# A gate column loaded as rows and turned by TensorE, and a re-searched order of operations, in a fused two-branch attention kernel

## The chip, the cores and the metric

One core of a Trainium2 chip. The metric is the device time of one execution in microseconds (us); the profile's span is about 1.7 us shorter than the time of the same execution. The profile shows five engines, and the program gives each its own fixed list of instructions: TensorE (PE, with its weight loads PEld), VectorE (DVE), ScalarE (ACT), GpSimd (POOL) and SyncE (SP), which issues most of this program's DMA. The lists are tied together by semaphores, and from these the profile infers what an engine waited for. A run counts as slow when it is over 1.5% above the fastest of its kernel in the same set; all others are called fast.

## The reference, cut to what matters

```
x = A_x                                            # 1 x 2048 x 640, bf16
g = sigmoid((x * gate_w).sum(-1, keepdims=True))   # one gate per token
a = A(x)   # linear attention, feature map softmax(+-x w), 32 heads of 20
b = B(x)   # 4 segments of 512 tokens: causal softmax attention + memory
return g * a + (1 - g) * b
```

The sum over `x * gate_w` is one more output column of a matrix product with x. The kernel therefore keeps `gate_w` as column 641 behind the 640 columns of the B branch's value weights.

## The kernel before

The program doesn't list its instructions in order. It builds a graph of some 1460 operations, each with its engine, an assumed duration and a priority, and a list scheduler in the same file turns the graph into one fixed order per engine and hands out PSUM banks. A table of offsets, found by a search, shifts the priorities:

```
NUDGE = {6: 1.6, 7: 1.65, 8: -2.2, ... 1450: -5.4}          # 417 entries (cut)
...
o.pr = pr + NUDGE.get(len(self.ops), 0.0)
...
# schedule(): per engine, among what is ready, the lowest priority number
# of those that could start within DELTA of the earliest
ch = min(((o.pr, o.idx, s, o) for s, o in cands if s <= lim))
```

The gate column was loaded by GpSimd, element by element, after the weight loads of B (`after=[last]`) and, in GpSimd's order, behind the building of masks:

```
self.WvB = fx("WvB", [128, NCH, D + 1], BF16)
...
self.dma("sp", self.WvB[:, :, 0:D], wsrc(ins["B_wv"]), W=[(self.WvB, "w")], pr=-760, dur=0.6, lat=5.6, name="WvB")
...
self.dma("pool", self.WvB[:, :, D:D + 1], ins["gate_w"].rearrange("(c p o) -> p c o", p=128, o=1),
         W=[(self.WvB, "g")], pr=-40, lat=6.0, noncontig=True, name="gw", after=[last])
```

and it is used by the value projection of each 128 tokens, whose operation reads both parts of the tile:

```
for kc in range(NCH):
    l = xT[:, kc, 128 * t:128 * (t + 1)]
    e.matmul(self.pf(pt, 0, 0, 512), lhsT=l, rhs=self.WvB[:, kc, 0:512], ...)
    r = e.matmul(self.pf(pt, 1, 0, 129), lhsT=l, rhs=self.WvB[:, kc, 512:641], ...)
```

The softmax here doesn't subtract the row's maximum and nothing guards it: scores larger than these inputs give would overflow.

## Time and profile before

| | before |
|---|---|
| time, median of the first 3 runs (range) | 337.8 us (336.91 to 338.0) |
| span of the profiled run | 334.1 us |
| TensorE busy / without a matmul | 303.6 / 30.5 us |
| VectorE, ScalarE busy | 244.5, 258.2 us |

"Without a matmul" is the span less TensorE's busy time. It is the quantity to watch, because both kernels do the same matmuls but one. The lines of the profile are shown in the prediction.

### The profile page before, as it was taken

The numbers are of one execution on the slowest core, as the hardware profiler recorded it, in microseconds if no ns is written. First come the engines' busy times: TensorE is split into PE (matmuls) and PEld (weight loads), VectorE is DVE, ScalarE is ACT, GpSimd is POOL, SyncE is SP. The second block draws the span as 40 slices with busy tenths as digits, with TensorE's granted clock in tenths as the row PEclk, the third lists the DMA queues.
The fourth block names the chain that finished last, engine by engine and source line by source line (L and its number), as shares of the span: only waits on it lengthen the run. The fifth ranks groups of instructions, "written<-read, shape, count | busy, mean of one in ns | idle before, by whom it ended". The sixth has DMA issues, their size and how long they took to land.

```text
span 334.1 us, 8947 instructions
## 1 busy us (share of the span) xinstructions
PE 303.6 (91%) x3836; PEld 176.2 (53%) x3836; DVE 244.5 (73%) x485; ACT 258.2 (77%) x325; POOL 114.8 (34%) x170
## 2 busy tenths in 40 slices
PE   7978999999987998899889999999999998889996
PEld 3434555476554545565454554664654655465763
DVE  4425898999999979899969798463792728667640
ACT  3448988978897898998977999768979776965522
POOL 6528323321434325642532114143221433322300
PEclk9999999999999999999999999999999999999999
DMA  7999992753722739650584104732014331210011
GB/s 248 302 142 222 81 146 56 79 119 57 104 39 45 117 54 88 122 97 2 121 157 41 22 1 62 129 70 61 22 22 57 84 59 33 50 42 22 22 41 59
DMA packets 68823, 27.52 MB, mean 82 GB/s; under 512 B 60400, under 2 KB 66864, under 8 KB 68784
## 3 DMA queue, kind: packets, MB, share of 16 engines
q1 hardware_dynamic: 68688, 26.92, 45.9%
q8 instruction: 30, 0.49, 0.6%
q0 software_dynamic: 96, 0.04, 0.3%
q14 instruction: 9, 0.07, 0.1%
HBM read 7.57 MB, written 4.59 MB: 36 GB/s over the span
## 4 chain that ended last, share of the span: by engine, by line
PE 45%; ACT 25%; DVE 15%; POOL 6%; DMA 6%; issue 2%; POOLq 0%; DVEq 0%
PE ps L1339 10%; ACT expT L999 6%; PE ps L1049 6%; ACT expT L1010 5%; PE ps L848 5%; ACT ET L1243 4%; POOL expT L1004 4%; PE ps L1136 4%; PE ps L989 3%; ACT expT L1022 3%; DMA WvB<-in_gate_w_dram 3%; PE ps L1238 3%; PE ps L1340 3%; PE ps L869 2%; DMA TT<-E 2%; ACT E L1143 2%
## 5 line engine op out<-in xcount | busy, mean ns | idle before, releaser
L1004 POOL TENSOR_SCALAR_AFFINE_SELECT expT<-expT 128x512 bf16<-128x512 bf16 x128 | 96.2, 754 | 187.4 <-ACT expT L999 80.8
L999 ACT ACTIVATE expT<-ps 128x1024 bf16<-128x1024 f32 x64 | 61.7, 1024 | 12.1 <-PE ps L989 11.7
L1010 ACT ACTIVATE expT<-ps 128x2048 bf16<-128x2048 f32 x32 | 60.0, 1875 | 4.9 <-PE ps L989 4.7
L1049 PE MATMUL ps<-v1B,expT 128*128 128x42 bf16 (+1 forms) x1280 | 42.3, 181 | 4.5 <-POOL expT L1004 2.7
L1049 PEld LDWEIGHTS ps<-v1B,expT 128*128 128x128 bf16 x1280 | 38.5, 96 | 12.5 <-POOL expT L1004 4.0
L848 PE MATMUL ps<-xT,WB 128*128 128x512 bf16 x175 | 42.0, 380 | 2.0 <-DVE KVZacc L1195 0.9
L989 PE MATMUL ps<-qk 20*128 20x384 bf16 (+3 forms) x512 | 34.5, 302 | 4.9 <-ACT expT L1010 2.4
L1022 ACT ACTIVATE expT<-ps 128x1024 bf16<-128x1024 f32 x32 | 32.7, 1023 | 5.5 <-PE ps L989 5.3
L816 ACT ACTIVATE out<-ps 128x640 bf16<-128x640 f32 x16 | 11.3, 704 | 25.1 <-PE ps L1340 24.9
L869 PE MATMUL ps<-WvB,xT 128*128 128x512 bf16 x80 | 23.9, 381 | 3.0 <-DMA WvB<-in_gate_w_dram 2.2
L848 PEld LDWEIGHTS ps<-xT,WB 128*128 128x128 bf16 x175 | 15.5, 98 | 21.0 <-DVE KVZacc L1195 1.2
L1154 DVE TENSOR_TENSOR E<-E,z 128x1280 bf16<-128x1280 bf16 x16 | 25.0, 1565 | 0.4
L1243 ACT ACTIVATE ET<-ps 128x512 bf16<-128x512 f32 x40 | 23.1, 598 | 2.8 <-PE ps L1238 2.2
L1339 PE MATMUL ps<-Wo,oTA 128*128 128x512 bf16 x80 | 23.6, 380 | 1.8 <-ACT expT L999 1.0
L1151 DVE TENSOR_REDUCE z<-E 128x64 f32<-128x1280 bf16 x16 | 23.7, 1479 | 1.8 <-ACT E L1143 1.8
L1136 PE MATMUL ps<-WkA,xT 128*128 128x512 bf16 x80 | 23.6, 380 | 1.1 <-ACT E L1143 0.6
L1136 PE MATMUL ps<-WvA,xT 128*128 128x512 bf16 x80 | 23.5, 380 | 1.0 <-ACT expT L999 0.5
L989 PEld LDWEIGHTS ps<-qk 20*128 20x128 bf16 x512 | 10.3, 91 | 26.6 <-ACT expT L1010 6.7
L1238 PE MATMUL ps<-xT,WqA 128*128 128x512 bf16 x100 | 23.9, 380 | 0.2 <-ACT ET L1243 0.2
L1143 ACT ACTIVATE E<-ps 128x640 bf16<-128x640 f32 x32 | 22.7, 709 | 1.8 <-PE ps L1137 1.2
L1339 PE MATMUL ps<-Wo,oTB 128*128 128x512 bf16 x80 | 23.4, 379 | 0.0
L1163 DVE TENSOR_TENSOR acc<-acc,TT 128x640 bf16<-128x640 bf16 x31 | 19.2, 618 | 3.8 <-DMA TT<-E 3.3
(132 smaller groups left out, 580.1 us busy)
## 6 DMA issues: line engine op xcount, KB each, us to landing
out_dram<-out SPq DMA_DIRECT2D x16, 160.0 KB, 1.9
scr<-qk SPq DMA_DIRECT2D x16, 120.0 KB
qk<-scr SPq DMA_DIRECT2D x16, 120.0 KB
stq<-in_B_wq_dram SPq DMA_DIRECT2D x5, 160.0 KB
WvB<-in_B_wv_dram SPq DMA_DIRECT2D x1, 800.0 KB, 5.3
WvA<-in_A_wqkv_dram SPq DMA_DIRECT2D x1, 800.0 KB, 9.7
Wo<-in_A_wo_dram SPq DMA_DIRECT2D x1, 800.0 KB
Wo<-in_B_wo_dram SPq DMA_DIRECT2D x1, 800.0 KB
```

The lines of the kernel that those rows point to most:

```text
L848: r = e.matmul(self.pf(pt, 0, 0, LSEG), lhsT=self.WB[:, w, kc, 128 * c:128 * (c + 1)], rhs=xT[:, kc, LSEG * n:LSEG * (n + 1)], start=(kc = ...
L869: e.matmul(self.pf(pt, 0, 0, 512), lhsT=l, rhs=self.WvB[:, kc, 0:512], start=(kc == 0), stop=(kc == 4))
L989: r = e.matmul(self.pf(pts[i][0], pts[i][1], c0, N), lhsT=qk[32 * i:32 * i + DH, g, 1, 128 * j:128 * (j + 1)], rhs=qk[32 * i:32 * i + DH, ...
L999: self.op("act", d_act(1024), lambda e, p=p, pt=pt: e.activation(ex[:, 2 * p:2 * p + 2, off:off + 512], self.pbanks(pt, 0, 2, 512), ACT.Ex ...
L1004: self.op("pool", d_pool(n_el), lambda e: e.affine_select(view(), view(), pattern=pat, compare_op=ALU.is_ge, fill=0.0, base=0, channel_mul ...
L1010: return e.activation(ex[:, :, off:off + 512].rearrange("p (k b) c -> p k b c", k=2), src, ACT.Exp, scale=scale)
L1022: return e.activation(ex[:, :, 1024:1280].rearrange("p (k b) c -> p k b c", k=2), src, ACT.Exp, scale=scale)
L1049: r = e.matmul(self.pf(ad, b, 84 * q2 + 21 * i, w) if n else self.pf(ad, 0, 84 * qi + 21 * i, w), lhsT=ex[:, i, c0:c0 + 128], rhs=vt[:, j, ...
L1136: e.matmul(self.pf(pt, 0, 0, 512), lhsT=l, rhs=W[:, kc, 0:512], start=(kc == 0), stop=(kc == 4))
L1238: r = e.matmul(self.pf(pt, 0, 0, LSEG), lhsT=self.WqA[:, kc, 128 * c:128 * (c + 1)], rhs=xT[:, kc, LSEG * S:LSEG * (S + 1)], start=(kc == ...
L1243: op("act", d_act(512), lambda e, s=s, ET=ET, pt=pt: e.activation(ET[:, s, :], self.pf(pt, 0, 0, LSEG), ACT.Exp, scale=1.0 - 2.0 * s), W=[ ...
L1339: e.matmul(self.pf(pt, 0, 0, 512), lhsT=l, rhs=self.Wo[:, c, 0:512], start=(c == 0), stop=(c == 9))
```

## The change

The intent: have the gate column in place early without a load of 640 single values and without GpSimd's queue; then search the order again, longer, with the two new operations in the graph.

```diff
-NUDGE = {6: 1.6, ... 1450: -5.4}      (417 entries)
+NUDGE = {6: 1.6, ... 1452: -5.4}      (601 entries; both cut)
-        self.WvB = fx("WvB", [128, NCH, D + 1], BF16)
+        self.WvB = fx("WvB", [128, NCH, D + 2], BF16)
+        self.gwr = fx("gwr", [NCH, 128], BF16)
-        self.dma("pool", self.WvB[:, :, D:D + 1], ins["gate_w"].rearrange("(c p o) -> p c o", p=128, o=1), ..., after=[last])
+        self.dma("sp", gwr[:, :], ins["gate_w"].rearrange("(c p) -> c p", p=128), W=[(gwr, "*")], pr=-790, dur=0.45, lat=6.0, name="gwr")
+        gt = self.pst("gw", 1)
+        op("pe", 0.1, lambda e: e.transpose(self.pb(gt, 0, 0, NCH), gwr[:, :], idt[0:NCH, 0:NCH]), ..., name="gwtr")
+        op("dve", 0.15, lambda e: e.tensor_copy(self.WvB[:, :, D], self.pb(gt, 0, 0, NCH)), ..., name="gwc")
```

## The prediction

> **What bounds the kernel now.** I read the page first, for the engines. Busy time over the span:
>
> ```profile
> PE 303.6 (91%) x3836; PEld 176.2 (53%) x3836; DVE 244.5 (73%) x485; ACT 258.2 (77%) x325; POOL 114.8 (34%) x170
> PEclk9999999999999999999999999999999999999999
> ```
>
> The reader is to see that TensorE (PE) is the fullest engine and that its clock is full in every slice, so nothing is to be gained or lost by the clock. The span is 334.1 us, so TensorE is without a matmul for 334.1 - 303.6 = 30.5 us. No reordering can save more than that as long as the matmuls stay the same.
>
> Second, the windows of 10 us over the whole span say where those 30.5 us lie. A few of them (columns: window, length, then busy us of PE, PEld, DVE, ACT, POOL with instruction counts, clock, DMA share, GB/s):
>
> ```profile
> 10.00:20.00 10.00, 8.79 (x41) 3.82 (x39) 2.34 (x5) 4.32 (x8) 3.46 (x6) 1.00 1.16 241
> 20.00:30.00 10.00, 7.83 (x74) 4.27 (x78) 3.93 (x7) 6.33 (x12) 6.82 (x12) 1.00 1.23 196
> 30.00:40.00 10.00, 10.00 (x81) 4.84 (x82) 8.21 (x19) 8.98 (x11) 5.75 (x11) 1.00 0.87 128
> ...
> 170.00:180.00 10.00, 7.85 (x122) 5.44 (x120) 8.36 (x21) 6.33 (x9) 3.48 (x4) 1.00 0.68 123
> 180.00:190.00 10.00, 10.00 (x60) 4.34 (x58) 8.58 (x18) 9.68 (x16) 2.97 (x3) 1.00 0.08 16
> ...
> 280.00:290.00 10.00, 8.02 (x122) 5.13 (x122) 7.55 (x19) 7.71 (x9) 2.55 (x4) 1.00 0.20 35
> ```
>
> The reader is to see that TensorE is idle in small portions everywhere: 1.9 us in the first window, 1.2 and 2.2 us in the next two, then between 0 and 2.2 us in each. Summed from 20 to 320 us it is 24.4 us. The last 14 us hold another 2.9, which is the last eviction (0.70 us) and the last store (1.9 us from issue to landing): a tail that no order removes.
>
> Third, the waits of TensorE by group, for the change's own target:
>
> ```profile
> PE ps L1049 <- POOL expT L1004: 2.7, 3, 1.0
> PE ps L989 <- ACT expT L1010: 2.4, 5, 0.8
> PE ps L869 <- DMA WvB<-in_gate_w_dram: 2.2, 1, 2.2
> ```
>
> Line 869 is the first value projection of the B branch; its weight tile WvB carries the gate column as column 641. It waits once, 2.2 us, for the gate load. The other waits are spread over many causes, none above 2.7 us in all.
>
> Fourth, the chain of waits up to 24 us, and the timeline of the same stretch:
>
> ```profile
> 10.76 0.40 POOL Mm L723
> 11.16 0.29 issue
> 11.46 9.41 DMA WvB<-in_gate_w_dram
> 20.87 0.14 issue
> 21.01 0.38 PE ps L869
> ```
>
> ```profile
> 17.76 1.03 PE L848 MATMUL ps<-xT,WB 128*128 128x512 bf16 x4
> 21.01 0.38 PE L869 MATMUL ps<-WvB,xT 128*128 128x512 bf16 x1 [2.22 <-DMA WvB<-in_gate_w_dram]
> ```
>
> The chain shows 9.41 us of DMA, but that is the length of the transfer, not the price. It was issued from GpSimd only at 11.46, after a row of mask-building selects on that engine, and landed at 20.87. TensorE had matmuls until 18.79. So the price is 21.01 - 18.79 = 2.2 us. Nothing is hidden behind it: in these 2.2 us VectorE waits too (it is idle from 15.3 until 22.2, when the w_phi load lands, and that load was issued from GpSimd just behind the gate load), and ScalarE has nothing from 19.4 to 22.6.
>
> **What the Trainium skill says.** DMA: Bandwidth & Descriptors, section Rules for kernel authors, says that a strided or non-contiguous last dimension "Lowers to one descriptor per element". The trace agrees in kind: the gate load is 640 separate values of 2 bytes, and its 1.2 KB take 9.4 us from issue to landing. But the same page's fixed cost (section Anatomy of one DMA, about 2.0 us) isn't reached by its neighbours either: beta takes 9.0 and w_phi 9.7 in the same crowd. The DMA engines are then at 1.16 to 1.23 of a share in the windows above, so I put much of the 9.4 us down to the crowd, not to the scatter. TensorE: Matmul & The Clock Gate, section Part 4: PE-mode transpose, says a transpose is a matmul against the identity whose result goes to PSUM and needs a copy after it. The trace has 20 such transposes of x in 1.28 us, 0.064 us each. Perfetto Trace Analysis, section Identifying the Most-Contended Engine, warns that matmul busy time is no measure of the distance to the peak; I use it for idle time alone.
>
> **The change part by part.** (1) Removed: the GpSimd gate load, 1.02 us of issue on GpSimd, and with it the 2.2 us of TensorE. w_phi and beta keep their place on GpSimd and move up by that 1.02 us, so the block matrix BD that needs w_phi could be ready about 1 us sooner.
>
> (2) Added: one load of five rows of 256 bytes on the SP queue, behind the weight pieces of B_wk and ahead of the w_k transpose. SP's copies take 2.38 us for 5 issues, 0.48 each, so every later SP issue moves back by about 0.5 us: the w_k transpose from 4.76 to 5.24, the WvB weights from 10.49 to about 11.0. The latter landed 5.3 us after issue, that is at 10.49 + 0.57 + 5.3 = 16.4 at the latest, and lands about 16.9 then. TensorE wants them at 18.8, so the shift is hidden. The row load itself should land with the weight pieces ahead of it, which let ScalarE go at 8.8 and 9.8: say at 10.
>
> (3) Added: one transpose of 5 x 128, about 0.06 us of TensorE, and one 128 x 5 copy from PSUM on VectorE, about 0.2 us by its smallest operations (0.18 us for 128 x 32). VectorE is idle between 10.5 and 13.4 and from 15.3 on, so the copy is free. If the transpose sits between the q projection (to 13.4) and the k projection, it costs 0.06 us. There is one risk: TensorE's order is fixed, so if it sits ahead of the landing it blocks what follows.
>
> The column is then in place by about 14 us, and the value projection can start at 18.8: saved 2.2 - 0.06, about 2.1 us. How much of it reaches the end? From 30 to 90 us TensorE is busy 58.2 of 60 us, so a shift at 20 us comes through to there; later, parts follow ScalarE or VectorE, whose work has been moved earlier by the same shift. I count 2.0 us.
>
> (4) Moved: the order. The table of priority offsets grows from 417 entries to 601. After correcting for the two operations inserted, 238 old entries are kept, 177 have another value and 186 are new, so about a quarter of some 1450 operations get another priority; durations, buffers and pool sizes stay. What it may reach is the idle time of TensorE between 20 and 320 us, 24.4 us less the 1.0 us of it that belongs to the gate wait: 23.4. How much of it the search gets, the profile can't say. The old order came from a search as well, so the easy part is gone; and the waits left are small and scattered, so they are partly timing noise of loads that a search doesn't see (one spread transpose of the A branch shows 7.96 us at 163.3 on the chain). My choice is 15%, 23.4 x 0.15 = 3.5 us.
>
> Sum: 2.0 + 3.5 = 5.5 us, on a median of 337.8: **332.0 us** after rounding down by 0.3 for the earlier w_phi.
>
> **The rivals.** (a) The gate wait is replaced by another: w_phi or WvB becomes last. For it: w_phi lands about a microsecond after the gate column and holds VectorE for 6.9 us. Against it: the value projection doesn't need w_phi, and QK matmuls are ready besides. Then the gain of part 1 is only about 1 us and the time 333 us or, if the search finds nothing, 336.5. (b) The order gains nothing on the chip, since a search works on predicted times and the chip's differ: 335.8 us. For it: the gate wait itself shows that such predictions miss, since the code gives that load 6.0 us where the trace has 9.4. Against it: the code's durations for engines are close (a 1024 exponential is given 0.94 us, the trace has 1.02; a value projection 1.38, the trace 1.38). (c) The order gains much: 35 to 40% of the idle time, 8 to 9 us, so 327 us; 184 more entries would hint at it. ScalarE at 77% and VectorE at 73% leave room; but from 40 to 100 us VectorE is busy 57.3 of 60 us, so there it is nearly the bound and an order gains little. (d) The transpose stands too early and stalls TensorE on the new load; that would cost up to 1 or 2 us and take back part 1.
>
> **Range and chances.** 2% of 337.8 is 6.8 us, so faster needs 331.0 or less; that takes 4.8 us from the order beside the 2.0, a fifth of the idle time. I think that somewhat less likely than not. Low end 326.5: rival (c) in full. High end 336.3: rivals (a) and (b) together. Slower would need an order that is wrong by over 8 us against its own prediction. Faster 0.41, same 0.56, slower 0.03.
>
> **What would show it.** In the changed profile: no wait of line 869 for a gate load, and the first value projection at 18.8 to 19.2; the gate rows landing before 13; TensorE's busy time within 1 us of 303.6; its idle time down to some 25 us, with the saving past 30 us scattered, not in one place; w_phi issued near 11.4. The prediction is wrong if TensorE is idle as long as before past 60 us (the order gave nothing), if the wait before the first value projection only changes its name, or if idle time falls below 21 us.

## More of the kernel before

One more view of the kernel before is needed later: what TensorE waited for between 60 and 116 us (columns: engine, tile and line that waited, releaser, total us, times, longest us).

```profile
PE ps L1184 <- ACT expT L999: 1.3, 1, 1.3
PE ps L1049 <- POOL expT L1004: 1.0, 1, 1.0
PE ps L848 <- DVE KVZacc L1195: 0.9, 1, 0.9
```

Three waits make 3.2 us in a stretch where VectorE is busy nearly all the time. Line 1184 is a product of the A branch, E transposed times V summed over four tiles (the K-V product), line 1049 the product of probabilities and values of the B branch, line 848 a Q or K projection.

## The result and the profile after

The changed kernel took 327.78 us (median of 4 runs, 327.46 to 328.59) against 337.9 us (4 runs, 336.91 to 339.37). The ratio is 0.970, 95% interval 0.966 to 0.974: faster. A ratio is the mean time of one kernel's fast runs over that of the other's fast runs of the same rounds, so it is not quite the ratio of the medians. A second set, with more rounds (e10 below), gave 327.64 against 335.29 us, ratio 0.977 (0.973 to 0.981): faster, but whether by 2% is unclear from this set alone. The median of the changed kernel repeats to 0.14 us; that of the kernel before doesn't. What is known of the reason is told with e10.

The page of the changed kernel:

```profile
span 326.8 us, 8901 instructions
PE 296.8 (91%) x3786; PEld 176.3 (54%) x3837; DVE 242.5 (74%) x485; ACT 258.9 (79%) x326; POOL 113.0 (35%) x169
```

The reader has to see a trap here. TensorE seems to have become 6.8 us less busy, but its matmul count is 3786 while its weight loads number 3837, one more than before: 51 matmul records are missing from this trace. The second trace of the same kernel (e10) is complete:

```profile
span 325.6 us, 8952 instructions
PE 302.0 (93%) x3837; PEld 175.8 (54%) x3837; DVE 243.7 (75%) x485; ACT 259.2 (80%) x326; POOL 113.1 (35%) x169
```

So TensorE's work is the same within 1.6 us, and its time without a matmul fell from 334.1 - 303.6 = 30.5 to 325.6 - 302.0 = 23.6 us. Of the 8.5 us between the two spans 6.9 are idle time of TensorE; the other 1.6 are busy time, and why that fell is open. Some windows of that complete trace (columns as in the prediction), and below them two of the kernel before:

```profile
10.00:20.00 10.00, 10.00 (x53) 4.28 (x50) 2.93 (x6) 6.03 (x11) 3.44 (x6) 1.00 1.13 277
20.00:30.00 10.00, 9.28 (x89) 4.88 (x88) 5.00 (x13) 9.00 (x13) 8.90 (x18) 1.00 1.03 199
30.00:40.00 10.00, 8.95 (x77) 5.02 (x74) 8.21 (x14) 7.83 (x12) 3.49 (x6) 1.00 0.95 116
90.00:100.00 10.00, 9.18 (x128) 5.78 (x125) 9.56 (x16) 8.90 (x11) 4.28 (x5) 1.00 0.34 63
100.00:110.00 10.00, 10.00 (x138) 5.46 (x136) 9.83 (x17) 8.76 (x12) 4.26 (x6) 1.00 0.27 52
```

```profile
90.00:100.00 10.00, 8.49 (x103) 4.87 (x102) 9.83 (x16) 9.63 (x13) 3.88 (x4) 1.00 0.27 53
100.00:110.00 10.00, 8.09 (x119) 5.00 (x116) 9.55 (x18) 6.67 (x8) 5.29 (x6) 1.00 0.36 67
```

Between 10 and 30 us TensorE is busy 19.3 us instead of 16.6, but between 30 and 40 us it is busy 8.95 instead of 10.00; between 90 and 110 us 19.2 instead of 16.6. The start, in the timeline of the first trace of the changed kernel:

```profile
4.75 0.41 SPq L687 DMA_DIRECT2D gwr<-in_gate_w_dram  x1
13.41 0.17 PE L730 MATMUL ps<-ident,gwr 5*128 5x5 bf16 x1
14.12 0.17 DVE L731 COPY WvB<-ps 128x5 bf16<-128x5 bf16 x1
16.86 0.40 PE L1009 MATMUL ps<-qk 20*128 20x512 bf16 x4
19.35 0.38 PE L889 MATMUL ps<-WvB,xT 128*128 128x512 bf16 x1
```

The rows are issued at 4.75; the turn at 13.41 waits for nothing (no "idle before" stands in its brackets); the value projection, line 889 now, starts without a wait. And the order is another one: the first QK product stands before the end of the K projection, at 16.86 instead of 22.48, so ScalarE's exponentials begin 6 us sooner.

### The profile page after: what moved, and what is told of

The parts are those of the page before. It is cut to its first block, busy times and chain, and to the rows that moved or that the text cites. A ratio compares the mean times of both kernels' runs of the same rounds, so it can differ in the third digit from the quotient of the medians.

```text
span 326.8 us, 8901 instructions
## 1 busy us (share of the span) xinstructions
PE 296.8 (91%) x3786; PEld 176.3 (54%) x3837; DVE 242.5 (74%) x485; ACT 258.9 (79%) x326; POOL 113.0 (35%) x169
## 4 chain that ended last, share of the span: by engine, by line
PE 47%; DVE 25%; ACT 20%; DMA 4%; issue 2%; POOL 1%; DVEq 0%
PE ps L1359 9%; PE ps L868 6%; PE ps L1069 6%; ACT expT L1030 5%; ACT ET L1263 4%; PE ps L1009 3%; ACT expT L1019 3%; PE ps L1360 3%; DVE E L1174 3%; PE ps L1258 3%; PE ps L889 2%; DMA TT<-E 2%; PE ps L1156 2%; DVE z L1171 2%; DVE acc L1183 2%
## 5 line engine op out<-in xcount | busy, mean ns | idle before, releaser
L868 PE MATMUL ps<-xT,WB 128*128 128x512 bf16 x165 | 40.5, 380 | 4.8 <-DVE KVZacc L1215 1.9
L836 ACT ACTIVATE out<-ps 128x640 bf16<-128x640 f32 x15 | 10.6, 704 | 24.3 <-PE ps L1360 24.3
L1258 PE MATMUL ps<-xT,WqA 128*128 128x512 bf16 x94 | 23.0, 380 | 1.1 <-DVE cs L1093 0.4
L1171 DVE TENSOR_REDUCE z<-E 128x64 f32<-128x1280 bf16 x16 | 23.6, 1477 | 0.2
L1156 PE MATMUL ps<-WvA,xT 128*128 128x512 bf16 x74 | 22.1, 379 | 0.0
L1156 PE MATMUL ps<-WkA,xT 128*128 128x512 bf16 x72 | 21.3, 380 | 0.6 <-ACT E L1163 0.6
L889 PE MATMUL ps<-WvB,xT 128*128 128x512 bf16 x72 | 21.7, 380 | 0.1
L1359 PE MATMUL ps<-Wo,oTA 128*128 128x512 bf16 x71 | 21.0, 380 | 0.7 <-DMA oTA<-oA 0.7
L1115 DVE TENSOR_TENSOR cb<-ps,cs 128x640 bf16<-128x640 f32 x24 | 19.7, 819 | 0.6
```

The source lines that it names most:

```text
L868: r = e.matmul(self.pf(pt, 0, 0, LSEG), lhsT=self.WB[:, w, kc, 128 * c:128 * (c + 1)], rhs=xT[:, kc, LSEG * n:LSEG * (n + 1)], start=(kc = ...
L1156: e.matmul(self.pf(pt, 0, 0, 512), lhsT=l, rhs=W[:, kc, 0:512], start=(kc == 0), stop=(kc == 4))
L1258: r = e.matmul(self.pf(pt, 0, 0, LSEG), lhsT=self.WqA[:, kc, 128 * c:128 * (c + 1)], rhs=xT[:, kc, LSEG * S:LSEG * (S + 1)], start=(kc == ...
L1359: e.matmul(self.pf(pt, 0, 0, 512), lhsT=l, rhs=self.Wo[:, c, 0:512], start=(c == 0), stop=(c == 9))
```

## The experiments

To separate the order from the gate, an order must be held still: a priority scheduler answers a small edit with another order everywhere. So each experiment but e10 (the changed kernel itself) replaces the scheduler's choice by a table of (operation, engine) recorded from one of the two kernels, and PSUM banks by the recorded ones (so "order" below means an order together with its banks; the two were not tested apart):

```diff
-                ch = min(((o.pr, o.idx, s, o) for s, o in cands if s <= lim))
+            for k, v in enumerate(todo):              # todo = list(ORDER), recorded
+                o, e = self.ops[v // 5], STREAMS[v % 5]
...
+            bs = forced.pop(0) if forced else bs      # banks as recorded
```

Line numbers of these kernels are shifted; the operations are named in the text.

### e1: the new gate path in the old order

```diff
 ORDER: before's, with
-  (gw, pool)
+  (gwr, sp) ahead of wkT; (gwtr, pe) ahead of the first K projection; (gwc, dve) behind the first q eviction
```

> The old order and the old PSUM banks, frozen; only the gate column arrives as in the changed kernel (five rows, turned by TensorE, copied). Theory T (the two parts add up): the gate wait is worth its 2.2 us, so about 335.8 against 337.9, and the order is worth the other 8. Rival R (the earlier column is what lets the rest move, so the parts are not separable): clearly more than 3 us here, 333 or less. Rival N (another wait takes the place): 337 or more, with a new wait in front of line 869's counterpart near 19 us.

Measured: 335.07 us (334.22 to 335.76, 4 runs) against 336.69 (7 runs), ratio 0.996 (0.991 to 1.001). By the times alone this can't be told from no gain: the interval includes 1, and three of the four runs had the clock dip of e10. In the trace the wait for the gate load is gone, and the first value projection follows the K projection.

```profile
17.91 0.38 PE L887 MATMUL ps<-xT,WB 128*128 128x512 bf16 x1
18.12 0.38 PE L908 MATMUL ps<-WvB,xT 128*128 128x512 bf16 x1
```

So the parts are separable, and the gate part is the small one. Rival R falls. Rival N falls as it was put, with a new wait near 19 us; but at 30 us TensorE waits 0.4 us for a copy of VectorE (WkA), which it didn't in the kernel before (see e5).

### e2: the new order with the old gate load

```diff
 ORDER: after's, without gwr, gwtr, gwc, with
+  (gw, pool) ahead of wphi       # the old scattered load, D + 1 columns
```

> The new order and the new PSUM banks, frozen; the gate column comes by the old scattered load from GpSimd, in front of w_phi. Theory T: the column lands at about 20.9, the new order wants it at 19.35, so 1.5 us are lost: about 329.3 against 327.8 of the changed kernel. Rival R: 332 or more, as the new order was built on the early column. Rival N: 327.8, no loss.

Measured: 329.67 us (327.91 to 331.76, 4 runs), ratio 0.982 (0.976 to 0.989). The number fits theory T, but for another reason than I wrote. Two of the four runs had the clock dip of e10 (329.64 and 331.76 us); the two at full clock took 328.8 us on average. And no loss is in the profiled run, which took 327.91 us: the same load, issued from the same place at nearly the same time (11.41 us against 11.46), landed in 6.0 us instead of 9.4, and the projection didn't wait:

```profile
19.04 0.38 PE L903 MATMUL ps<-WvB,xT 128*128 128x512 bf16 x1
```

This made the 2.2 us of the first profile suspect, and e5 took another sample.

### e3 and e4: the scattered load, only sooner, in the old order

```diff
 e3:  -  dma("pool", WvB[:, :, D:D+1], <640 single values>, after=[last])
      +  dma("sp",   WvB[:, :, D:D+1], <640 single values>)      # where e1 issues its rows
 e4:  +  the same load as GpSimd's first instruction, no after=[last]
```

> The old order and banks; the gate column stays a scattered load of 640 values but is issued from SP where the five rows are issued in the changed kernel. If only the early issue matters, as e1: about 335.8. If the scatter itself is the cost (640 descriptors on the queue), the w_k transpose and WvB behind it are issued later by several us and the time is 337 or more.

> The old order and banks; the gate column stays a scattered load from GpSimd, issued as GpSimd's first instruction at about 0.5 us and without the wait for the B_wk load. If only the late issue was wrong, as e1: about 335.8, no TensorE work added. If the scatter crowds the first loads (xr, B_wq), the first transposes start later than 5.7 us and the gain is lost: 337 to 339.

Measured: e3 334.92 us (333.08 to 335.81), e4 334.75 us (332.62 to 336.55), ratios 0.995 (0.989 to 1.001) and 0.995 (0.988 to 1.002); e1 had 0.996. None of the three is clear of 1, so the times show neither a gain nor a difference between them. In the traces all three are rid of the wait: the projection starts at 17.88 us (e3), 18.00 (e4) and 18.12 (e1). The scatter costs nothing that shows: SP's issue takes 0.47 us where the five rows take 0.41 to 0.48, and the GpSimd load of e4 landed 6.0 us after its issue at 1.3 us. What removed the wait was the early issue. The rows, the turn and the copy are one way to it and not a better one.

### e5: the kernel before once more, as a control

```diff
 ORDER: before's, nothing changed
```

> A control: the kernel before, its order frozen in a table, instruction for instruction the same. The ratio should be 1.000 within 0.005. Its trace is a second sample of the gate load: theory L (the load's 9.4 us were one draw; in the order-only run the same load landed in 6.0) expects a landing below 9 us and a wait of TensorE below 2.2 us; the rival (the 9.4 belong to the old kernel) expects 9 us and 2.2 us again.

Measured: 334.41 us against 336.04, ratio 0.999 (0.993 to 1.006): the frozen table is the same kernel. The wait in front of its first value projection:

```profile
19.05 0.38 PE L903 MATMUL ps<-WvB,xT 128*128 128x512 bf16 x1 [0.27 <-DMA WvB<-in_gate_w_dram]
```

Theory L holds: 0.27 us here, 2.22 in the first trace, with landings after 7.5 and 9.4 us. The wait whose removal gave the change its name is a matter of each execution. The weights of the value projection were loaded at 20.98, 19.02 and (new gate path, e1) 17.91 us.

Nor does all of an earlier start come through. The two traces have the same instructions, so they can be compared one by one: e5 leads the first trace by 1.95 us at 25 us and by 1.14 us at 35 us. What took the 0.8 us is a wait that the first trace doesn't have, for VectorE's copy of a product out of PSUM:

```profile
PE ps L837 <- DVE WkA L851: 0.8, 1, 0.8
```

The same wait is 0.8 us in e3, 0.4 in e1 and 0.2 in e4.

### e6 and e7: each half of the new order

```diff
 e6:  ORDER = after's operations that start before 115 us, then before's order for the rest
 e7:  ORDER = before's operations that start before 115 us, then after's order for the rest
      (both with the new gate path; the two sets of operations differ by a handful)
```

> The new gate path; the new order for the 568 operations that start before 115 us, the old order for the rest (the two orders have then done the same work up to a handful of operations). The lead of the changed kernel over the kernel before, by matmul work done, was 5.6 us at that place and 7.4 at the end. Theory F (gains add, front-loaded): 5 to 6 us under the kernel before, about 331 to 332. Rival (the gain lies in the late part, the front only shifts): 335, as e1.

> The opposite half: the new gate path, the old order before 115 us and the new order after. Theory F: the gate's 1.5 to 2.2 us plus the late 1.8 us, so 333 to 334. Rival: 329 or less, if the late part carries most.

Measured: e6 331.63 us (329.45 to 331.93), e7 332.31 us (330.79 to 333.2) against 336.04; ratios 0.988 (0.982 to 0.995) and 0.991 (0.985 to 0.998). Both halves gain, and about equally, which is flatter than theory F had it. The traces say it more sharply than the times. Three marks from each trace (when TensorE loaded the weights, up to 0.2 us before the matmul, of the first value projection, the second K-V product, and one of its last matmuls), and the two stretches between them:

```
kernel                      value proj.  2nd K-V   last matmul   stretch 1  stretch 2
before                         20.98      99.12      330.62        78.1       231.5
e5  before again               19.02      97.75      328.63        78.7       230.9
e1  old order, new gate        17.91      96.36      328.99        78.5       232.6 *
e7  old, then new              18.62      98.12      327.40        79.5       229.3
e6  new, then old              19.06      94.38      326.33        75.3       232.0 *
e2  new order, old gate        18.82      94.69      322.71        75.9       228.0
after                          19.14      94.83      323.34        75.7       228.5
e10 after again                18.27      94.11      322.16        75.8       228.1
(* contains a dip of the granted clock worth 1.6 us, see e10)
```

With the old order stretch 1 takes 78.1 to 79.5 us, with the new 75.3 to 75.9: about 2.9 us less, and e6 has all of it. With the old order stretch 2 takes 230.9 to 231.5 us (the starred ones come to 231.0 and 230.4 without the dip), with the new 228.0 to 228.5: about 2.9 us less; e7 has 2 of them. What precedes stretch 1 holds the gate's part: 20.98 or 19.02 us with the late load in the old order, 17.9 (e1) to 19.1 with the new path. From e5 to e10 0.75 us of the 6.5 lie there.

### e8: the new order with the early scattered load

```diff
 ORDER: after's, without gwr, gwtr, gwc, with
+  (gw, pool), (wphi, pool), (beta, pool) as GpSimd's first instructions, after=[last] removed from all three
```

> The new order without the turn on TensorE: the scattered gate load, then w_phi and beta, are the first three instructions of GpSimd and wait for nothing. If early issue is all that matters: equal to the changed kernel, 327 to 328. If the row load with its transpose is needed: 329 or more. A gain is possible, as GpSimd no longer waits for the beta load (6.7 us): at best 326.5.

Measured: 327.81 us (327.19 to 328.56), ratio to before 0.979 (0.972 to 0.986). Equal to the changed kernel within the noise, so the turn on TensorE isn't needed with the new order either; and that GpSimd's wait for the beta load (6.7 us in the changed kernel) is gone gained nothing that shows.

### e9: one local move in the old order

The profile puts the 1.3 us in front of the K-V product down to ScalarE. VectorE's timeline in the kernel before shows another candidate:

```profile
92.66 1.75 DVE L1163 TENSOR_TENSOR acc<-acc,TT 128x640 bf16<-128x640 bf16 x2
97.52 1.48 DVE L1154 TENSOR_TENSOR E<-E,z 128x1280 bf16<-128x1280 bf16 x1
99.15 2.66 PE L1184 MATMUL ps<-vA,E 128*128 128x140 bf16 x40 [1.33 <-ACT expT L999]
```

(two views, VectorE's and TensorE's timeline.) The normalisation of E, which the product reads, ended at 99.00, and accumulations that nobody waits for soon stood ahead of it. (In the lists below acc are these accumulations; Zsum, Zrec and Anorm the row sums of E, their reciprocals and the normalisation; tmp, cf and cmb belong to other steps.)

```diff
 VectorE's order (as e1 otherwise):
-  acc, acc, tmp, cf, Zsum, Zrec, cmb, cmb, cmbp, Anorm
+  Zsum, Zrec, cmb, cmb, cmbp, Anorm, acc, acc, tmp, cf
```

> As e1 (old order, new gate path), but on VectorE alone four operations nobody waits for soon (two of the acc chain, one tmp, one cf; 1.9 us together) are moved behind the normalisation of E that the K-V product of the A branch needs. In the kernel before, TensorE stood 1.33 us in front of that product at 97.8 us; the profile names ScalarE's exponential as the releaser, but VectorE's normalisation ended at the same moment. Theory V (VectorE's order set that wait): the wait falls to 0.3 us or less and the lead over the kernel before grows by 1.0 to 1.3 us there; time about 1 us under e1. Rival A (the exponential set it): still 1.3 us there, same time as e1.

Measured: 333.76 us (333.15 to 334.8), ratio 0.995 (0.989 to 1.000). The waits of TensorE between 60 and 116 us, first e1, then e9:

```profile
PE ps L1223 <- ACT expT L1038: 1.3, 1, 1.3
PE ps L887 <- DVE KVZacc L1234: 0.9, 1, 0.9
PE ps L1088 <- POOL expT L1043: 0.9, 1, 0.9
```

```profile
PE ps L887 <- DVE KVZacc L1234: 2.2, 1, 2.2
PE ps L1175 <- ACT E L1182: 0.6, 2, 0.4
PE ps L1088 <- DVE v1B L856: 0.4, 1, 0.4
```

The wait at the K-V product is gone, although ScalarE's order is the same: VectorE's order had set it, and not the releaser that the profile names. The trace confirms theory V for that wait. It doesn't become time in this stretch: the projection that follows now waits 2.2 us for VectorE's accumulation of the same product, where it had waited 0.9, as VectorE is nearly full here. The 3.1 us of the three waits became 2.2. Compared instruction by instruction, e9 was 1.65 us behind e1 before the product (for reasons earlier in the trace), 0.28 behind at it, and 1.74 behind at the projection after it: the 1.4 us that were won were lost at once. The times can't add to this, as all four runs of e9 had a clock dip, in the profiled one just after this place. In the same stretch the changed kernel (e10, 56 to 113 us) has only this:

```profile
PE ps L868 <- DVE KVZacc L1215: 0.8, 1, 0.8
PE ps L1156 <- ACT E L1163: 0.6, 2, 0.4
```

The searched order is rid of the other two large waits as well, which one move wasn't; which of its many moves did that isn't shown.

### e10: the changed kernel again, with the clock of every run

No edit.

> The changed kernel unaltered, five rounds against the kernel before, with the granted clock of every run of both. Theory C (part of the 10 us between the first medians was a short clock dip, seen as a granted clock of 0.994 to 0.995 and worth about 1.6 us, in the runs of the kernel before): among runs at full clock the difference is 6 to 8 us, and runs of the kernel before at 0.995 are 1.5 to 2 us slower than its others. Rival: 10 us at equal clock too.

Measured: 327.64 us (326.52 to 328.57, 6 runs) against 335.29 (332.92 to 338.38, 11 runs), ratio 0.977 (0.973 to 0.981). The mean granted TensorE clock of the runs:

| kernel | clock 0.999 or 1.0 | clock 0.990 to 0.995 |
|---|---|---|
| before (the 23 fast runs in the rounds of e1 to e11, three chips) | 335.06 us (16 runs) | 336.72 us (7 runs) |
| after (10 runs, two sets) | 327.74 us (10 runs) | none |

Theory C holds: at full clock the difference is 7.3 us, and a run of the kernel before with a dip is 1.7 us slower on average. Two more of its runs with a dip (338.07 us at 0.995, 338.38 at 0.990) count as slow and are left out. The dip can be seen in the profiled run of e1 (columns as in the other windows; the clock is the third number from the right):

```profile
285.00:291.00 6.00, 5.20 (x122) 3.71 (x119) 3.54 (x10) 5.91 (x8) 1.53 (x3) 1.00 0.28 55
291.00:296.00 5.00, 4.43 (x28) 2.11 (x25) 3.14 (x6) 1.65 (x2) 1.90 (x3) 0.66 0.02 5
296.00:302.00 6.00, 5.44 (x76) 3.27 (x75) 4.31 (x10) 2.64 (x3) 0.63 (x1) 1.00 0.09 30
```

```profile
292.51 0.63 PE L1378 MATMUL ps<-Wo,oTA 128*128 128x512 bf16 x1
293.04 0.63 PE L1378 MATMUL ps<-Wo,oTA 128*128 128x512 bf16 x1
...
295.17 0.38 PE L1378 MATMUL ps<-Wo,oTB 128*128 128x512 bf16 x1
295.44 0.38 PE L1378 MATMUL ps<-Wo,oTB 128*128 128x512 bf16 x1
```

From 292.0 to 295.1 us a pair of output matmuls takes 0.53 us, afterwards 0.27: half speed for 3.1 us, that is 1.6 us lost. Kernels with the old order in the second half (before, e1, e3, e4, e5, e6, e9) had it in 23 of 49 runs, those with the new one (after, e2, e7, e8, e11) in 4 of 28 (slow runs counted too). That the order makes it rarer is suggested by these counts, not shown; what triggers it stays open. The clocks of the very first runs of the kernel before, with the median of 337.9, aren't recorded; so the rest of the 10.1 us between the first medians can't be assigned. The profiled run of that kernel is recorded: 335.83 us at 0.999, in line with the table.

### e11: two more moves, in the new order

The changed kernel still had two waits of the kind that e9 showed: at 31 us a projection waited for a q eviction that stood on VectorE behind seven small gate operations, and at 167 us the last K-V product waited because VectorE stood in front of two accumulations whose transposed operand hadn't landed, with the normalisation behind them.

```diff
 VectorE's order (as the changed kernel otherwise):
-  eg, g, omg, cf, cf, cf, cf, qk_ev, WkA, qk_ev, WkA, tmp, qk_ev
+  qk_ev, eg, g, omg, WkA, cf, qk_ev, WkA, cf, tmp, qk_ev, cf, cf
 ...
-  acc, acc, Anorm, cmb, cmb, cmb, cmbp, cmba
+  Anorm, cmb, cmb, cmb, cmbp, cmba, acc, acc
```

> The changed kernel's order with two groups of VectorE operations moved, nothing else: the seven small gate operations at 28.3 us (2.9 us in a row) are spread behind the qk eviction that TensorE waits 1.16 us for, and two acc operations that wait for a spread transpose at 162 us (2.4 us) go behind the normalisation that the last K-V product waits 1.36 us for. If such waits are the path: 1.5 to 2.5 us under the changed kernel, about 325.5 to 326.3. Rival (another wait takes their place): 327.3 to 328.

The waits, of the changed kernel (first trace; TensorE twice, then VectorE):

```profile
PE ps L868 <- DVE qk L837: 1.2, 1, 1.2
PE ps L1204 <- DVE cs L1093: 1.4, 1, 1.4
DVE acc L1183 <- DMA TT<-E: 2.4, 1, 2.4
```

Measured: 325.7 us (324.81 to 327.43, 6 runs), on the chip and in the rounds where the changed kernel had 327.64; ratio to the kernel before 0.971 (0.967 to 0.975), against 0.977. All three waits are gone from its trace, and the page shows where the time came from:

```profile
span 323.9 us, 8951 instructions
PE 301.9 (93%) x3837; PEld 175.8 (54%) x3837; DVE 242.8 (75%) x485; ACT 259.2 (80%) x326; POOL 112.8 (35%) x169
```

TensorE's time without a matmul is 22.0 us, after 23.6. Two hand moves gave 1.9 us more, and this is the fastest version. The gain falls where the moves are: compared instruction by instruction, e11 leads e10 by 0.5 us from 34 to 163 us and by 1.6 us after the K-V product, at 172 us.

## Why the prediction was right or wrong

The time, 327.8 us, lies inside the range (326.5 to 336.3), near its low end; the case called most likely was a change within 2%, and it was faster by 2.3 to 3.0%. The direction was right, and that both parts gain; the term of the order was sized too small, and part of the miss in the time comes from the base.

**The bound.** Right. TensorE's work stayed the same and its idle time fell from 30.5 to 23.6 us; the prediction looked for some 25. (Its last 14 us hold 3.0 us of that, not 2.9.) That nothing was to be lost by the clock holds for the profiled run alone: other runs had the dip of e10.

**The gate wait, "price" 2.2 us, 2.0 counted.** The size holds roughly, the reasoning doesn't. One profile gave the price, and the price differs by execution: 2.22 us in one trace, 0.27 in another. On average e1, e3 and e4 in their five runs at full clock took 333.7 us, against 335.1 for the kernel before at full clock (335.9 for its four such runs on the same chip): 1.4 to 2.2 us, which runs that differ by 2 us among themselves don't fix more closely. That such a shift comes through from 30 us on was too simple: of 1.95 us in e5, 1.14 were left (the wait for WkA). That the crowd of loads made much of the 9.4 us isn't shown: issued at 1.3 us, beside the first loads, it still took 6.0 us (e4) and 5.7 (e8), issued at 11.4 us 6.0 to 9.4, so its later place in the crowd made 0 to 3.7 us of it. The scatter isn't what makes it long either: w_phi and beta, issued right behind it in e8, took 5.6 and 5.9 us.

**Added work.** Right. The w_k transpose is issued at 5.21 us (predicted 5.24), WvB at 10.63 (11.0) and it landed at about 16.0 (16.9); the turn and the copy have records of 0.17 us each and nobody waited for them. Rival (d), a turn that stalls TensorE, did not occur. Rival (a), another load in the place of the first, did not occur as it was put: TensorE had no wait for a load there. But in the old order a wait for VectorE, of 0.2 to 0.8 us, took part of its place.

**The order, 15% of 23.4 us, so 3.5.** This is the term that was too small, and its reason is the step that failed: "the waits left are small and scattered, so they are partly timing noise of loads that a search doesn't see", and the 15% chosen from it. What the runs showed in its place: at full clock the change is worth 335.06 - 327.74 = 7.3 us; less 1.4 to 2.2 for the gate leaves 5.1 to 5.9 us, or 22 to 25% of the same 23.4. The marks give the same: 2.9 us in stretch 1 and 2.9 in stretch 2. So do traces with the gate column early in both orders, compared at equal matmul work: e10 leads e4 by 0.7 us at 90 us, 3.2 at 115 and 5.3 at the end, and e8 leads e3 likewise by 1.1, 3.5 and 5.3. The waits were small but not noise: the 1.33 us before the K-V product stands in every trace with the old order there (before, e1, e3, e4, e5, e7). Three of the larger ones have one cause that the list of waits spreads over several names: VectorE's fixed order puts something nobody needs yet ahead of something TensorE needs. e9 showed it for one wait of the old order, e11 for two that the new order still had. That the search won its 5 to 6 us in this way is not shown: e9's move alone gave no time, and no run has the new order on VectorE alone. Rival (b) falls with e2, e6 and e7; (c) came nearer, though at 22 to 25% and not 35 to 40%. My argument that VectorE is nearly the bound from 40 to 100 us, so an order gains little there, was wrong in its conclusion: stretch 1, with its gain of 2.9 us, lies mostly there. VectorE's total is hardly reduced (244.5 to 243.7 us); but in e9 and e11 what it did first decided whether TensorE stood.

**The base.** I subtracted from 337.8 us, the median of three runs. The kernel before has 16 later runs at full clock with a mean of 335.06. From that base the same gain of 5.5 us would have given 329.6: of the 4.2 us between 332.0 and 327.8, about 2.4 come from the base and 1.8 from the gain. It could have been seen: the span of the profiled run, 334.1 us, is that of a run of 335.8 us, 2 us below the median that I subtracted from.

**Checks named in advance.** No wait of the value projection for a gate load: so. It starts at 18.8 to 19.2: 19.35 and 18.48 in the two traces, just outside on either side. The gate rows landing before 13: the landing isn't recorded, but in e10 the turn ran at 12.53 us without a wait. Busy time within 1 us of 303.6: 302.0 in the complete trace, 1.6 off. Saving past 30 us scattered: in part; both halves have some, but by the leads above nearly half of the order's gain falls between 90 and 115 us. w_phi issued near 11.4: 11.46.

## What to carry to other kernels

A wait read from one profile is one draw: before removing a wait for a load, look at a second trace, and first try to issue the same load sooner, which here removed the wait as well as a cleverer load. On an in-order engine that is 75% busy, look for operations that nobody needs yet, above all those that themselves wait for a transfer, standing ahead of what the bounding engine waits for; moving two such groups gave 1.9 us even after a long search. Hold the order fixed in a table when testing an edit in a scheduled program, and compare marks in the traces as well as times.

## What the Trainium skill lacked or had wrong

- DMA: Bandwidth & Descriptors, Anatomy of one DMA, gives about 2.0 us fixed plus the bytes. At the crowded start of this kernel a load of 1.2 KB landed 9.4, 7.5 and 6.0 us after issue in three traces (before, e5, e2) with nearly the same loads around it, and 6.0 and 5.7 us when issued first (e4, e8); the section gives no figure for a load behind others, nor that it varies by execution.
- DMA: Bandwidth & Descriptors, Rules for kernel authors, says to rearrange a non-contiguous last dimension. For 640 values it made no difference that shows here: 334.92 and 334.75 us scattered, 335.07 as rows; SP's issue 0.47 against 0.41 to 0.48 us. Its "one descriptor per element" agrees with the packets of the load from SP (69344 in queue q1 in e3, 68688 in the kernel before); for the load from GpSimd the profile has only 32 packets (96 in queue q0 with it, 64 without).
- TensorE: Matmul & The Clock Gate, Part 4: PE-mode transpose, has about 390 ns in isolation and 275 in a kernel for 128 x 128. Here each of the 20 transposes of x has a record of 219 ns, and as they overlap the 20 take 1.28 us, 64 ns each; the record of the smaller 5 x 128 turn is 173 ns.
- The same page, Why this matters for your kernels, names idle gaps of over about 3 us as what brings the clock to half. In e1 the clock halved for 3.1 us where the gap just before was 0.57 us, in a run at 0.995 on average; that row alone doesn't account for it.
- Perfetto Trace Analysis, Identifying the Most-Contended Engine, warns of matmul busy time, but not that matmul records can be missing from a profile: here 51 of 3837 in one trace, in which TensorE looks 5.2 us less busy than in the complete trace of the same kernel (296.8 against 302.0).
